# Splitting an x pair over two PSUM banks, five lead units, an earlier close of st0 and a last block in three column pieces, in a fused attention and feed-forward kernel

## The chip, the cores and the metric

One Trainium2 chip, one core of it. The metric is the device time of one execution in microseconds (us), which is about 1.7 us more than the span of the profile (287.74 for a profiled span of 286.0). Times are medians.

## The reference

Inputs are q, k, v of shape (8, 8, 576, 64) in float32, w_in (512, 2048), w_out (2048, 512) and beta (2048).

```python
q_s = softmax(q, axis=-1)             # over the head dimension
k_s = softmax(k, axis=2)              # over the sequence
kv  = einsum('bhsd,bhse->bhde', k_s, v)
x   = einsum('bhsd,bhde->bhse', q_s, kv)      # then (B*S, H*D) = (4608, 512)
h   = x @ w_in
out = (h * sigmoid(beta * h)) @ w_out
```

## The kernel before

The matmuls run in bf16. The 4608 tokens go through the feed-forward part in nine chunks of 512. A *unit* is 128 of the 2048 hidden columns of one chunk: four matmuls (k steps 0 to 3) into one PSUM bank, a tanh on ScalarE, and one VectorE instruction that makes g. The second matmul collects in *acc groups*: for each of the four 128-token slices st0 to st3 of a chunk, 16 matmuls go into one bank, which is then stored. `b_mm(m)` issues the next m acc matmuls of a fixed list, but none whose g is newer than four units (LAG). The attention of batch b+1 runs between the units of chunk b; batches 0 and 1 stand alone, in the code below. In the traces of this case each engine works in the order in which its instructions are written (in e7_exp_first below, one line moved up takes the Exp ahead of a copy on ScalarE, from 49.47 to 48.91 us).

```python
    def h_bank(n, i):                          # PSUM bank of unit i of chunk n
        if n == 0:
            return ("H0", "H1", "H2", "A0", "A1")[i % 5]
        if n == 1 and i < 6:
            return ("H0", "A0", "H1", "H2", "X0", "X1")[i]
        return f"H{(n * NJ + i + 2) % 3}"
    # the list of acc matmuls, chunk 1 and later
        for j in range(0, NJ, 4):
            for st in (0, 1):
                bq += [(n, st, j + m) for m in range(4)]
        for st in (2, 3, 4)[: 2 + (n == NCH - 1)]:
            bq += [(n, st, j) for j in range(NJ)]
    # ... (cut: b_mm, store) batch_1, its second half:
        b_mm(2)
        for i in range(4):
            unit_mm(1, i, 0, 1)                # k step 0 of units 0 to 3
        kv_pair(1, 3, "K")
        kv_mask(1, 3)                          # VectorE: gives kvp(1,3)
        x_mm(1, 2, "X0")
        q_exp(2, 0, 4)                         # ScalarE: Exp for batch 2
        x_out(1, 2, nc.scalar)
        q_exp(2, 4, 8)
        for i in range(4):
            unit_mm(1, i, 1, 2)
        x_mm(1, 3, "X1")
        x_out(1, 3, nc.vector, 0, 2)           # two copies out of one bank
        x_out(1, 3, nc.scalar, 2, 4)
        # ... (cut)
        for i in range(4):
            unit_mm(1, i, 2, 3)
```

In chunks 1 to 8 st0 and st2 share bank A1, st1 and st3 bank A0. In the last block st3 is done in two pieces of 256 columns, and the second is copied out by ScalarE and then VectorE, 128 columns each.

The softmax here doesn't subtract the row's maximum and nothing guards it: scores larger than these inputs give would overflow.

## Time and profile before

| | before |
|---|---|
| time, median of 3 runs | 288.08 us (287.67 to 288.71) |
| span of the profile | 286.0 us |
| TensorE busy | 97% |
| a 512-column matmul, start to start | 0.216 us |

Three lines of the page: the span, the engines' busy time, and the chain of waits by engine.

```profile
span 286.0 us, 4210 instructions
PE 277.5 (97%) x1445; PEld 132.4 (46%) x1472; DVE 158.9 (56%) x303; ACT 169.5 (59%) x275; POOL 79.2 (28%) x135
...
PE 83%; DMA 12%; POOL 1%; issue 1%; SPq 1%; ACT 1%; DVE 0%; ACTq 0%; POOLq 0%
```

TensorE is the bottleneck nearly everywhere, so the useful reading is not its busy share but its gaps. In a list of matmul starts, a 512-column matmul is followed by the next after 0.216 us; whatever is beyond that is a wait. (Exactly 0.216 more is taken as a missing record, unless another engine's record ends just before the later matmul starts.) The timeline has fewer gaps than that list: it gives a gap only when an engine was idle by its records, and there a 512-column matmul counts as busy for 0.38 us, 0.16 us longer than its slot. So add 0.16 us to a gap in brackets to have the time lost. (One gap, 0.45 us at 45.9 us for a cast of v, is left alone by the change.)

**Batch 0.** The timeline of TensorE, and of POOL (GpSimd), which casts the weights w_in. Columns: start, length, engine, line, operation, out and in, shapes, count, and in brackets the idle time and who ended it.

```profile
15.40 7.52 PE L405 MATMUL h<-xT,w_in_b 128*128 128x512 bf16 x31
23.25 6.65 PE L405 MATMUL h<-xT,w_in_b 128*128 128x512 bf16 x30 [0.32 <-POOL w_in_b L154]
```

```profile
16.38 1.18 POOL L154 TENSOR_SCALAR_AFFINE_SELECT w_in_b<-wi 128x512 bf16<-128x512 f32 x2 [0.75 <-DMA wi<-in_moe_w_in_dram]
...
21.21 1.05 POOL L154 TENSOR_SCALAR_AFFINE_SELECT w_in_b<-wi 128x1024 bf16<-128x1024 f32 x1 [0.67 <-DMA wi<-in_moe_w_in_dram]
```

POOL waited for the loads of w_in before each cast, and TensorE waited for POOL at 23.25. The stretch is paced by loads.

**Batch 1, second half.** TensorE, ScalarE (ACT) and VectorE (DVE):

```profile
49.07 1.03 PE L405 MATMUL h<-xT,w_in_b 128*128 128x512 bf16 x4
50.35 1.89 PE L405 MATMUL h<-xT,w_in_b 128*128 128x512 bf16 x8 [0.25 <-ACT xT L145]
52.23 0.39 PE L453 MATMUL acc<-w_out_b,g 128*128 128x512 bf16 x1
```

```profile
48.98 1.06 ACT L182 ACTIVATE Eq<-q 128x1024 bf16<-128x1024 f32 x1 [0.20 <-DMA q<-in_q_dram]
49.94 0.35 ACT L145 CAST xT<-x 128x256 bf16<-128x256 f32 x1
```

```profile
46.87 0.68 DVE L485 TENSOR_SCALAR o<-acc 128x512 f32<-128x512 f32 x1
47.97 0.17 DVE L320 RECIPROCAL rks<-kv 128x1 f32<-128x1 f32 x1 [0.43 <-PE kv L310]
...
49.27 0.42 DVE L159 CAST xT<-x 128x256 bf16<-128x256 f32 x1 [0.74 <-PE x L360]
```

The matmuls at 50.35 are the closing k steps of the lead units. They wait for ScalarE's half copy at 49.94, which stands behind an Exp of 1.06 us, and that Exp waited for a load of q: 0.415 us lost. The first acc matmul of chunk 1 (52.23) starts 0.154 us late, because g(1,0) had only just been made.

**A bank wait in the steady chunks.** TensorE near 104.6, then ScalarE:

```profile
104.63 1.18 PE L453 MATMUL acc<-w_out_b,g 128*128 128x512 bf16 x4
```

```profile
103.57 0.36 ACT L145 CAST xTt<-xt 128x256 bf16<-128x256 f32 x1
103.83 0.64 ACT L182 ACTIVATE Eq<-q 128x512 bf16<-128x512 f32 x1
104.36 0.60 ACT L487 ACTIVATE o<-acc 128x512 f32<-128x512 f32 x1
```

Four matmuls took 1.18 us in place of 1.03 (0.16 us lost), because st2 takes the bank of st0, whose store (104.36 to 104.95) is late behind a copy and an Exp. The same stands at 134.6 and 164.7, and 0.04 us at 74.7.

**The tail,** after the last matmul, which starts at 282.49:

```profile
282.85 0.28 ACT L479 ACTIVATE o_4b<-acc 128x128 f32<-128x128 f32 x1 [2.94 <-PE acc L453]
283.15 0.38 ACTq L482 DMA_DIRECT2D out_dram<-o_4b  x1
283.15 0.29 DVE L473 TENSOR_SCALAR o<-acc 128x128 f32<-128x128 f32 x1 [1.68 <-ACT o_4b L479]
```

VectorE's copy waits for ScalarE's copy of the same bank, and its DMA is the last to be issued.

### The profile page before, as it was taken

What the parts mean: (1) busy time and instruction counts of PE and PEld (TensorE: products, weight loads), DVE (VectorE), ACT (ScalarE), POOL (GpSimd) and SP (SyncE); (2) the same over time, 40 slices, a digit from 0 to 9 for tenths busy, and PEclk for the clock granted to TensorE, in tenths of its full rate; (3) what the DMA queues carried; (4) which work ended last, traced back from release to release, by engine and by line L of the source; (5) the groups of instructions that cost most, each with busy time, mean ns of one, the idle gap of its engine ahead of it and who ended that gap; (6) DMA issues with size and microseconds to landing.
All of it is one profiled execution on the core that took longest, in us unless ns stands there. A gap on an engine that the chain in (4) does not pass through costs nothing.

```text
span 286.0 us, 4210 instructions
## 1 busy us (share of the span) xinstructions
PE 277.5 (97%) x1445; PEld 132.4 (46%) x1472; DVE 158.9 (56%) x303; ACT 169.5 (59%) x275; POOL 79.2 (28%) x135
## 2 busy tenths in 40 slices
PE   8899999999999999999999999999999999999995
PEld 3443445454454444544454445444544444444444
DVE  5857346976856484747574666557553344433301
ACT  4767268956965588358835785568554544354421
POOL 7578953540531045103610271016100000000000
PEclk9999999999999999999999999999999999999999
DMA  7999999979589907990699059902400111031112
GB/s 234 353 364 386 381 355 353 361 207 360 142 205 351 161 37 194 364 198 2 161 359 269 2 135 310 308 2 89 99 37 0 73 39 38 0 75 39 37 73 73
DMA packets 55782, 51.67 MB, mean 181 GB/s; under 512 B 21184, under 2 KB 48208, under 8 KB 55760
## 3 DMA queue, kind: packets, MB, share of 16 engines
q1 hardware_dynamic: 55584, 51.33, 59.3%
q8 instruction: 11, 0.18, 0.3%
q14 instruction: 11, 0.09, 0.1%
q10 hardware_dynamic: 176, 0.07, 0.1%
HBM read 38.28 MB, written 9.44 MB: 167 GB/s over the span
## 4 chain that ended last, share of the span: by engine, by line
PE 83%; DMA 12%; POOL 1%; issue 1%; SPq 1%; ACT 1%; DVE 0%; ACTq 0%; POOLq 0%
PE h L405 40%; PE acc L453 39%; DMA v<-in_v_dram 5%; DMA q<-in_q_dram 4%; DMA wi<-in_moe_w_in_dram 3%; PE kv L283 2%; PE x L360 2%; SPq L132 1%; POOL w_out_b L154 0%; ACT Eq L182 0%; PE xt L375 0%; ACT th L417 0%; POOL w_in_b L154 0%; SPq L122 0%; POOL k L119 0%
## 5 line engine op out<-in xcount | busy, mean ns | idle before, releaser
L419 DVE SCALAR_TENSOR_TENSOR g<-th,h 128x512 bf16<-128x512 bf16 x144 | 98.2, 686 | 97.5 <-ACT th L417 97.3
L417 ACT ACTIVATE th<-h,beta_h 128x512 bf16<-128x512 f32 x144 | 98.4, 688 | 89.4 <-PE h L405 86.5
L453 PE MATMUL acc<-w_out_b,g 128*128 128x512 bf16 (+1 forms) x573 | 142.5, 373 | 0.9
L405 PE MATMUL h<-xT,w_in_b 128*128 128x512 bf16 x507 | 129.1, 379 | 0.9 <-POOL w_in_b L154 0.3
L405 PEld LDWEIGHTS <-w_in_b 128*128 128x128 bf16 x576 | 56.1, 98 | 69.2 <-POOL w_in_b L154 1.9
L453 PEld LDWEIGHTS <-g 128*128 128x128 bf16 x592 | 56.9, 98 | 62.7 <-issue 1.0
L194 POOL TENSOR_TENSOR Eq<-Eq,qz 128x512 bf16<-128x512 bf16 (+1 forms) x26 | 30.6, 1180 | 90.8 <-DVE qz L191 71.4
L182 ACT ACTIVATE Eq<-q 128x512 bf16<-128x512 f32 (+1 forms) x26 | 18.9, 727 | 10.7 <-DMA q<-in_q_dram 10.7
L190 DVE TENSOR_REDUCE qz<-Eq 128x8 f32<-128x512 bf16 (+1 forms) x27 | 21.0, 778 | 7.3 <-ACT Eq L182 7.3
L252 ACT ACTIVATE Ek<-k 128x640 bf16<-128x640 f32 (+1 forms) x30 | 22.9, 769 | 1.6 <-DMA k<-in_k_dram 1.3
L487 ACT ACTIVATE o<-acc 128x512 f32<-128x512 f32 x34 | 20.1, 595 | 6.1 <-PE acc L453 6.1
L154 POOL TENSOR_SCALAR_AFFINE_SELECT va<-v 128x256 bf16<-128x256 f32 (+1 forms) x55 | 20.7, 417 | 3.6 <-DMA v<-in_v_dram 3.6
L405 PE MATMUL h<-xTt,w_in_b 128*128 128x512 bf16 x62 | 16.2, 379 | 0.1
L360 PE MATMUL x<-qT,kvp 128*128 128x512 bf16 x32 | 12.0, 379 | 0.2
L145 ACT CAST xT<-x 128x512 bf16<-128x512 f32 (+1 forms) x19 | 10.6, 558 | 1.1 <-PE x L360 0.6
L159 DVE CAST xT<-x 128x512 bf16<-128x512 f32 (+1 forms) x15 | 9.7, 648 | 1.6 <-PE x L360 1.6
L236 POOL TENSOR_TENSOR Et<-Et,zt 128x512 bf16<-128x512 bf16 x4 | 4.2, 1043 | 22.4 <-ACT th L417 11.4
L154 POOL TENSOR_SCALAR_AFFINE_SELECT w_in_b<-wi 128x512 bf16<-128x512 f32 (+2 forms) x16 | 9.5, 617 | 3.1 <-DMA wi<-in_moe_w_in_dram 3.1
L544 PE MATMUL warm<-zero 128*128 128x512 bf16 x26 | 8.1, 471 | 1.3 <-DVE zero L507 1.3
L283 PEld LDWEIGHTS <-Ek 128*128 128x128 bf16 x120 | 7.8, 97 | 2.8
L283 PE MATMUL kv<-va,Ek 128*128 128x130 bf16 x120 | 8.8, 220 | 0.0
L154 POOL TENSOR_SCALAR_AFFINE_SELECT w_out_b<-wo 128x1024 bf16<-128x1024 f32 x8 | 8.3, 1043 | 1.4 <-DMA wo<-in_moe_w_out_dram 1.4
(53 smaller groups left out, 76.8 us busy)
## 6 DMA issues: line engine op xcount, KB each, us to landing
k<-in_k_dram SPq DMA_DIRECT2D x28, 320.0 KB, 6.5
v<-in_v_dram SPq DMA_DIRECT2D x26, 320.0 KB, 7.2
q<-in_q_dram SPq DMA_DIRECT2D x16, 512.0 KB, 5.2
out_dram<-o SPq DMA_DIRECT2D x31, 256.0 KB, 2.4
wo<-in_moe_w_out_dram SPq DMA_DIRECT2D x8, 512.0 KB, 10.8
wi<-in_moe_w_in_dram SPq DMA_DIRECT2D x7, 512.0 KB, 8.5
out_dram<-o SPq DMA_DIRECT2D x9, 128.0 KB, 2.3
k<-in_k_dram SPq DMA_DIRECT2D x4, 256.0 KB, 7.0
```

Source lines behind the costliest of these rows:

```text
L154: nc.gpsimd.affine_select(out=dst, in_=src, pattern=[[0, n]], base=0, channel_multiplier=0, compare_op=ALU.is_equal, fill=fill0,)
L182: nc.scalar.activation(Eq[b][:, :, h0:h1, :].rearrange("p t h d -> p h t d"), ld["q", b, hf][:, a : a + h1 - h0, :].rearrange("p h (t d) - ...
L190: nc.vector.tensor_reduce(qz[b][:, :, h], Eq[b][:, :, h, :], axis=AX.X, op=ALU.add)
L194: eng.tensor_tensor(Eq[b][:, t0:t1, h0:h1], Eq[b][:, t0:t1, h0:h1], qz[b][:, t0:t1, h0:h1].unsqueeze(3).to_broadcast((P, t1 - t0, h1 - h0, ...
L252: nc.scalar.activation(Ek[b][:, :, h0:h1, :].rearrange("p t h d -> p h t d"), ld["k", b, hf][:, a : a + h1 - h0, :].rearrange("p h (t d) - ...
L283: nc.tensor.matmul(kvs[b, j // 2][:, j % 2, :], Ek[b][:, t, 2 * j : 2 * j + 2, :].rearrange("p h d -> p (h d)"), va[b % 2][:, t, j, :], st ...
L360: nc.tensor.matmul(xps[b, j][:], kvp[b][:, j, :], qT[b][:, :, j, :], start=True, stop=True)
L405: nc.tensor.matmul(hs[n, i][:], w_in_b[:, kt, i * P : (i + 1) * P], rhs_a(n, kt), start=(kt == 0), stop=(kt == KT - 1),)
L417: nc.scalar.activation(th[:], h[:], ACTF.Tanh, scale=beta_h[:, i : i + 1])
L419: nc.vector.scalar_tensor_tensor(out=g[:], in0=th[:], scalar=1.0, in1=h[:], op0=ALU.add, op1=ALU.mult)
L453: nc.tensor.matmul(acc[n, st][:, c0:c1], gs[n, j][:, min(st, 3) * P : (min(st, 3) + 1) * P], w_out_b[:, j, c0:c1], start=(j == 0), stop=(j ...
L487: nc.scalar.activation(o[:], acc[n, st][:], ACTF.Copy, scale=0.5)
```

## The change

The intent: take away these waits. (a) The last x pair of batches 0 and 1 is computed into two banks, so that two engines can copy at once. (b) In batch 1 the last key-value pair comes two matmuls earlier, and the last x pair behind two matmuls of k step 1 in place of four; the store of acc(0,3) goes behind its mask, the second Exp behind the half copies, and five units instead of four lead. (c) st0 closes sooner: two groups of st1 (eight acc matmuls) stand between its close and st2, where it was one, so that st2 finds its bank free. (d) The last block is done in pieces of 256, 128 and 128 columns in three banks. Cut to its core:

```diff
+    def x_split(b, j, na, nb):
+        # ... (cut)
+        for i, (n, eng) in enumerate(((na, nc.vector), (nb, nc.scalar))):
+            t = slice(2 * i, 2 * i + 2)
+            ps = bank(n, [P, 2, P], F32, f"x{b}_{j}_{i}")
+            nc.tensor.matmul(ps[:], kvp[b][:, j, :], qT[b][:, t, j, :], start=True, stop=True)
+            cast(eng, xT[b][:, j, t], ps[:])
 # h_bank
-            return ("H0", "H1", "H2", "A0", "A1")[i % 5]
-        if n == 1 and i < 6:
-            return ("H0", "A0", "H1", "H2", "X0", "X1")[i]
-        return f"H{(n * NJ + i + 2) % 3}"
+            return ("H1", "H2", "A0", "A1", "H0")[i % 5]
+        if n == 1 and i < 7:
+            return ("H0", "A0", "H1", "H2", "A1", "X0", "X1")[i]
+        return f"H{(n * NJ + i + 1) % 3}"
 # the list of acc matmuls
-        for j in range(0, NJ, 4):
-            for st in (0, 1):
-                bq += [(n, st, j + m) for m in range(4)]
-        for st in (2, 3, 4)[: 2 + (n == NCH - 1)]:
+        for st, j in ((0, 0), (1, 0), (0, 4), (1, 4), (0, 8), (0, 12), (1, 8), (1, 12)):
+            bq += [(n, st, j + m) for m in range(4)]
+        for st in (2, 3, 4, 5)[: 2 + 2 * (n == NCH - 1)]:
 # b_mm: st0 and st2 now in A0, st1 and st3 in A1; columns of the last block
+        if n == NCH - 1 and st > 2:
+            return ((0, DM // 2), (DM // 2, 3 * DM // 4), (3 * DM // 4, DM))[st - 3]
 # batch 0
-    x_mm(0, 3, "K")
-    x_out(0, 3, nc.vector, 0, 2)
-    x_out(0, 3, nc.scalar, 2, 4)
-    LEAD = (2, 4)
+    x_split(0, 3, "K", "H0")
+    LEAD = (2, 5)
 # batch 1
-        for i in range(4):
+        for i in range(2):
             unit_mm(1, i, 0, 1)
         kv_pair(1, 3, "K")
         kv_mask(1, 3)
+        store(0, 3)
+        for i in range(2, 4):
+            unit_mm(1, i, 0, 1)
         x_mm(1, 2, "X0")
         q_exp(2, 0, 4)
         x_out(1, 2, nc.scalar)
+        for i in range(2):
+            unit_mm(1, i, 1, 2)
+        x_split(1, 3, "X1", "K")
         q_exp(2, 4, 8)
-        for i in range(4):
+        for i in range(2, 4):
             unit_mm(1, i, 1, 2)
-        x_mm(1, 3, "X1")
-        x_out(1, 3, nc.vector, 0, 2)
-        x_out(1, 3, nc.scalar, 2, 4)
+        unit_mm(1, 4, 0, 2)
 # ... (cut: acc(0,3) is no longer stored right behind its last matmul;
 # k steps 2 and 3 of units 0 to 4 follow unit by unit; no b_mm after unit 4;
 # the store of the last block: pieces 1 and 2 on VectorE, piece 3 on ScalarE and its own DMA queue)
```

More of the change, by code (lines that the diff above doesn't have):

```diff
@@ L362, in x_mm @@
         )
+    def x_split(b, j, na, nb):
+        if b not in xT:
+            xT[b] = atn.tile([P, KT, NT, P], BF16, tag="xT", name=f"xT{b}")
+        for i, (n, eng) in enumerate(((na, nc.vector), (nb, nc.scalar))):
[3 more added lines that the diff above has]
+            cast(eng, xT[b][:, j, t], ps[:])
     def x_out(b, j, eng, t0=0, t1=NT):
@@ L439, with cols @@
     done_a = [-1]
+    def cols(n, st):
+        if n == NCH - 1 and st > 2:
+            return ((0, DM // 2), (DM // 2, 3 * DM // 4), (3 * DM // 4, DM))[st - 3]
+        return 0, DM
     def b_mm(m):
@@ L446, in b_mm @@
             if j == 0:
-                name = (f"A{1 - st % 2}", ("X1", "K", "A0", "A1", "")[st])[n == 0]
+                name = ("X1", "K", "A0", "A1")[st] if n == 0 else f"A{st % 2}"
+                if st == 5:
+                    name = "X0"
                 acc[n, st] = bank(name, [P, DM], F32, f"acc{n}_{st}")
-            c0, c1 = 0, DM
-            if n == NCH - 1 and st > 2:
-                c0, c1 = (st - 3) * DM // 2, (st - 2) * DM // 2
+            c0, c1 = cols(n, st)
             nc.tensor.matmul(
@@ L459, in b_mm @@
             )
-            if j == NJ - 1:
+            if j == NJ - 1 and (n, st) != (0, 3):
                 store(n, st)
@@ L468, in store @@
             rows = out[(B - 1) * S : (B - 1) * S + CH, :].rearrange("(p t) e -> p t e", t=NT)
-            for i in range(st - 2):
-                w = DM // 2 // (st - 2)
-                c0 = (st - 3) * DM // 2 + i * w
-                if st == 3 or i:
-                    nc.vector.tensor_scalar(
-                        o[:, c0 : c0 + w], acc[n, st][:, c0 : c0 + w], 0.5, None, op0=ALU.mult
-                    )
-                    nc.sync.dma_start(rows[:, 3, c0 : c0 + w], o[:, c0 : c0 + w])
-                else:
-                    o2 = osp.tile([P, DM], F32, tag="o", name=f"o{n}_{st}b")
-                    nc.scalar.activation(
-                        o2[:, 0:w], acc[n, st][:, c0 : c0 + w], ACTF.Copy, scale=0.5
-                    )
-                    nc.scalar.dma_start(rows[:, 3, c0 : c0 + w], o2[:, 0:w])
+            c0, c1 = cols(n, st)
+            if st < 5:
+                nc.vector.tensor_scalar(
+                    o[:, c0:c1], acc[n, st][:, c0:c1], 0.5, None, op0=ALU.mult
+                )
+                nc.sync.dma_start(rows[:, 3, c0:c1], o[:, c0:c1])
+            else:
+                nc.scalar.activation(o[:, c0:c1], acc[n, st][:, c0:c1], ACTF.Copy, scale=0.5)
+                nc.scalar.dma_start(rows[:, 3, c0:c1], o[:, c0:c1])
             return
@@ L656, in batch_1 @@
         x_out(1, 2, nc.scalar)
+        for i in range(2):
+            unit_mm(1, i, 1, 2)
+        x_split(1, 3, "X1", "K")
         q_exp(2, 4, 8)
-        for i in range(4):
+        for i in range(2, 4):
             unit_mm(1, i, 1, 2)
-        x_mm(1, 3, "X1")
-        x_out(1, 3, nc.vector, 0, 2)
-        x_out(1, 3, nc.scalar, 2, 4)
+        unit_mm(1, 4, 0, 2)
         q_sum(2, 0, 4)
         q_div(2, 0, NT, nc.gpsimd, 0, 4)
-        for i in range(4):
-            unit_mm(1, i, 2, 3)
     hooks: dict = {}
@@ L715 @@
         for i in range(NJ):
-            unit_a(n, i, 3 if n < 2 and i < LEAD[n] else 0)
+            unit_a(n, i, 3 - n if n < 2 and i < LEAD[n] else 0)
             for f in hooks.get((n, i), []):
                 f()
-            if n:
+            if n and (n, i) != (1, 4):
                 b_mm(4)
```

## The prediction

> **What bounds the kernel.** TensorE. On the page, PE is busy 97% of a 286.0 us span, PEclk is at full speed in every slice, and the chain of waits is 83% PE. In the timeline a 512-column matmul follows the one before every 0.216 us; I read each start gap beyond that as a wait (gaps of exactly 0.216 are missing records). From 52.5 us to the last matmul (ends 282.8) I find only about 0.5 us of waits. Everything to be gained lies in four places.
>
> 1. Batch 0, 15 to 23 us. The last x pair (one bank) is copied by VectorE (15.60 to 16.03), and only then by ScalarE (16.06 to 16.44), so the closing matmuls of units 0 and 1 start 0.22 us late. The Trainium skill (PSUM - Partial Sum Buffer, "PSUM bank collisions raise a hardware error") says two engines may not read one bank at once; the trace agrees in that ScalarE starts 0.03 us after VectorE ends. Two banks remove this wait. But unit 2 starts at 17.05 because POOL's w_in_b cast ends at 17.00, itself begun when its DMA landed; the same at 22.32 and 23.25 (gap 0.49). These are set by the loads. Expected gain: 0.
>
> 2. Batch 1, 42 to 52 us. Gaps of 0.29, 0.16, 0.45 (casts of v, Eq normalisation) are before the changed part and stay. Then 0.415 us at 49.9: the second half of the last x pair waits for a 1.06 us Exp on ScalarE and for VectorE, whose chain had been held by the 0.68 us store of acc(0,3). And 0.154 us at 52.07: the first acc matmul of chunk 1 waits for g(1,0) (ends 52.17). The change puts the key-value pair two matmuls earlier, the store behind its mask, the Exp behind the half copy, and unit 4 (20 matmuls of k steps 0 to 3) before the first acc matmul. Replayed with the trace's durations, xT(1,3) is ready near 49.3 and wanted at 49.7; g(1,0) is ready near 51.8 and wanted at 52.5. Gain 0.55.
>
> 3. Steady chunks. Gaps of 0.16 at 104.6, 134.6, 164.7 and 0.04 at 74.7: st2 takes the bank of st0 only 8 matmuls after st0 closed, with ScalarE late (xT tail cast, Exp, then the 0.60 us store). Closing st0 two groups sooner, more than 12 matmuls ahead, removes them. Gain 0.5. The acc queue lags four matmuls more, which moves work, not its amount. st1 now meets st3's bank after 8 matmuls (1.73 us), next to no ScalarE cast: fine.
>
> 4. Tail, after the last matmul: ScalarE copy 0.28, then VectorE copy 0.29 of the same bank, then SyncE's DMA (issue at 283.47, landed 285.1). Now one ScalarE copy and its own DMA issue (before: at 283.15). Gain 0.3. The 256-column piece becomes two 128-column pieces: 16 matmuls at 0.109 become 32 at 0.056 (the trace's pace for 128 columns), cost 0.05.
>
> **Sum:** 0 + 0.55 + 0.5 + 0.25 = 1.3 us of 288.08. Predicted 286.8 us, 80% range 285.9 to 287.8. Faster by over 2%: 1%; within 2%: 98%; slower by over 2%: 1%.
>
> **What would show it.** Span near 284.7; unit 2 of chunk 0 still near 17.05 and the 0.49 gap near 22.5 still there; no PE gap at 49 to 52 us and none between acc matmuls near 104, 134, 164; only a ScalarE copy after the last matmul, and the end about 3.0 us after it instead of 3.2.
>
> **What would make it wrong.** A new wait: units of chunk 1 taking PSUM banks still held by the moved store (unit 4 in A1, slack 0.2 us), ScalarE late in chunk 1 where acc matmuls are fewer, weight loads limiting the 128-column pieces (then up to 1.3 us more, from 97 ns per load), or w_in landing at other times.

## More of the kernel before

All runs told here were with a granted TensorE clock of 0.99 or 1.00.

VectorE's store of acc(0,3) (46.87) is over at 47.55, and VectorE then idles 0.43 us until the key-value pair's matmuls are done, so it holds nothing up.

**Start of chunk 2** (no gap here before the change; shown because one comes).

```profile
67.61 0.38 PE L360 MATMUL x<-qT,kvp 128*128 128x512 bf16 x1
67.83 1.03 PE L453 MATMUL acc<-w_out_b,g 128*128 128x512 bf16 x4
68.69 1.03 PE L405 MATMUL h<-xT,w_in_b 128*128 128x512 bf16 x4
```

## The result, and the profile after

| | before | after |
|---|---|---|
| time, median of 4 runs each, same rounds | 287.93 us | 287.21 us |
| range | 287.67 to 288.71 | 287.02 to 287.61 |
| span of the profile | 286.0 us | 285.5 us |

The ratio is 0.9972, with a 95% interval of 0.995 to 0.9995: about 0.8 us faster, and by the interval anything from 0.1 to 1.4 us. A ratio is the mean time of one kernel's fast runs over that of the other's of the same rounds, so not quite the ratio of the medians in the table.

```profile
span 285.5 us, 4276 instructions
PE 279.2 (98%) x1490; PEld 133.3 (47%) x1490; DVE 157.8 (55%) x303; ACT 169.5 (59%) x275; POOL 79.4 (28%) x135
...
PE 82%; DMA 14%; POOL 1%; SPq 1%; issue 0%; ACT 0%; POOLq 0%; ACTq 0%
```

Batch 0, TensorE and POOL. The wait at 16.71 stands where the two-bank copies have made room, and the waits before 22.67 and 23.61 are the loads'. The bracket at 22.67 names VectorE; but that bank had been freed by g of unit 3 at 20.06, and what ended at 22.61 was POOL's cast of the 1024-column weights. POOL had waited 1.36 us for them.

```profile
16.71 5.35 PE L415 MATMUL h<-xT,w_in_b 128*128 128x512 bf16 x24 [0.20 <-POOL w_in_b L154]
22.67 0.60 PE L415 MATMUL h<-xT,w_in_b 128*128 128x512 bf16 x2 [0.61 <-DVE g L429]
23.61 6.65 PE L415 MATMUL h<-xT,w_in_b 128*128 128x512 bf16 x30 [0.33 <-POOL w_in_b L154]
```

```profile
21.57 1.04 POOL L154 TENSOR_SCALAR_AFFINE_SELECT w_in_b<-wi 128x1024 bf16<-128x1024 f32 x1 [1.36 <-DMA wi<-in_moe_w_in_dram]
```

Batch 1: TensorE runs through from 48.79 to 53.3 without a gap. ScalarE's half copy is the second of the two at 48.55, ahead of the Exp; VectorE's store now stands behind the mask.

```profile
48.79 0.38 PE L371 MATMUL x<-qT,kvp 128*128 128x256 bf16 x2
49.00 4.05 PE L415 MATMUL h<-xT,w_in_b 128*128 128x512 bf16 x18
52.89 0.59 PE L467 MATMUL acc<-w_out_b,g 128*128 128x512 bf16 x2
```

```profile
48.55 1.02 ACT L145 CAST xT<-x 128x512 bf16<-128x512 f32 x2
49.47 1.06 ACT L182 ACTIVATE Eq<-q 128x1024 bf16<-128x1024 f32 x1
```

```profile
48.38 0.68 DVE L494 TENSOR_SCALAR o<-acc 128x512 f32<-128x512 f32 x1
49.10 0.42 DVE L159 CAST xT<-x 128x256 bf16<-128x256 f32 x1
```

Start of chunk 2, TensorE, then the copies of xT(2) on VectorE and ScalarE:

```profile
67.41 0.38 PE L360 MATMUL x<-qT,kvp 128*128 128x512 bf16 x1
67.62 0.38 PE L467 MATMUL acc<-w_out_b,g 128*128 128x512 bf16 x1
67.84 1.36 PE L415 MATMUL h<-xT,w_in_b 128*128 128x512 bf16 x4
```

```profile
67.64 0.68 DVE L159 CAST xT<-x 128x512 bf16<-128x512 f32 x1
```

```profile
68.19 0.58 ACT L145 CAST xT<-x 128x512 bf16<-128x512 f32 x1
```

This is new. Before, four acc matmuls (67.83 to 68.69) stood between the last x matmul and the first unit of chunk 2; now there is one, and the unit takes 1.36 us in place of 1.03, because its k steps 2 and 3 wait for the copies that end at 68.32 and 68.77.

The bank wait is gone (four matmuls in 1.03 us again), and after the last matmul, which now starts at 282.20, there is one copy:

```profile
103.85 1.03 PE L467 MATMUL acc<-w_out_b,g 128*128 128x512 bf16 x4
```

```profile
282.50 0.28 ACT L490 ACTIVATE o<-acc 128x128 f32<-128x128 f32 x1 [2.98 <-PE acc L467]
282.81 0.38 ACTq L491 DMA_DIRECT2D out_dram<-o  x1
```

From the last matmul's start to the end it is 3.26 us, before 3.53.

**The sum,** read from the starts of the same instructions in the two profiles:

| stretch | predicted | profiles (before to after) |
|---|---|---|
| batch 0, to the first acc matmul | 0 | +0.36 (29.73 to 30.09) |
| batch 1 | -0.55 | -0.57 (0.415 and 0.154 gone) |
| start of chunk 2 | 0 | +0.33 (new) |
| bank waits | -0.5 | -0.52 (3 x 0.16 and 0.04 gone) |
| last block and tail | -0.25 | -0.18 |
| all | -1.3 | -0.58; the spans differ by 0.57 |

Two terms have to be explained: the loss in batch 0, and the loss at the start of chunk 2.

### The profile page after: what moved, and what is told of

Its sections match the earlier page's. It is cut to its first block, busy times and chain, and to the rows that moved or that the text cites. A ratio compares the mean times of both kernels' runs of the same rounds, so it can differ in the third digit from the quotient of the medians.

```text
span 285.5 us, 4276 instructions
## 1 busy us (share of the span) xinstructions
PE 279.2 (98%) x1490; PEld 133.3 (47%) x1490; DVE 157.8 (55%) x303; ACT 169.5 (59%) x275; POOL 79.4 (28%) x135
## 4 chain that ended last, share of the span: by engine, by line
PE 82%; DMA 14%; POOL 1%; SPq 1%; issue 0%; ACT 0%; POOLq 0%; ACTq 0%
PE acc L467 39%; PE h L415 39%; DMA wo<-in_moe_w_out_dram 4%; DMA q<-in_q_dram 4%; PE kv L283 2%; DMA k<-in_k_dram 2%; DMA v<-in_v_dram 2%; DMA wi<-in_moe_w_in_dram 2%; PE x L360 2%; SPq L124 0%; PE xt L385 0%; POOL va L154 0%; SPq L122 0%; PE kv L310 0%; ACT xT L145 0%
## 5 line engine op out<-in xcount | busy, mean ns | idle before, releaser
L467 PE MATMUL acc<-w_out_b,g 128*128 128x512 bf16 (+2 forms) x608 | 145.0, 368 | 0.0
L360 PE MATMUL x<-qT,kvp 128*128 128x512 bf16 x30 | 11.2, 379 | 0.2
L553 PE MATMUL warm<-zero 128*128 128x512 bf16 x27 | 9.2, 509 | 1.2 <-DVE zero L516 1.2
```

Source lines behind the costliest of these rows:

```text
L360: nc.tensor.matmul(xps[b, j][:], kvp[b][:, j, :], qT[b][:, :, j, :], start=True, stop=True)
L467: nc.tensor.matmul(acc[n, st][:, c0:c1], gs[n, j][:, min(st, 3) * P : (min(st, 3) + 1) * P], w_out_b[:, j, c0:c1], start=(j == 0), stop=(j ...
```

## The experiments

My theory: the loss in batch 0 is scatter in the landing of loads and not the change's doing; the loss at chunk 2 comes with the new order of the acc groups; the gain in batch 1 comes from the moves, not from the two banks. Rivals: the split of batch 0 causes its loss; the five lead units cause the loss at chunk 2; the two banks, or the store's place, give the gain in batch 1. Ratios are to the kernel before, measured in the same rounds on the same chip. All eleven kernels gave correct results.

### 1. The change's parts alone

**e1_batch1**: only (b), with the split in batch 1, the banks for five lead units and the swap of A0 and A1; the order of the acc groups, batch 0 and the last block as before.

> Only the batch 1 part of the change (key-value pair earlier, store behind its mask, Exp behind the half copy, split banks, five lead units). Theory: the two TensorE gaps of 0.415 and 0.154 us between 49 and 53 us go, no new gap appears in chunk 1, and the time falls by 0.55 us (ratio 0.998). The gaps of 0.16 us in the later chunks (near 104, 134, 164 us) and the 3.53 us from the last matmul's start to the end stay. Rival (the gain of batch 1 is only pushed to a later wait): gaps of the same size turn up between 55 and 75 us and the time is that of before. The start of unit 8 of chunk 0, set by the loads, lies anywhere from 22.2 to 22.8 us, though nothing in batch 0 has changed.

Measured: 287.55 us, ratio 0.9985 (0.997 to 0.9999). Both gaps are gone, none is new, the three bank waits of 0.16 us and the tail of 3.54 us stay. As the theory said. Batch 0, untouched, ends 0.3 us later than in the profile of before (first acc matmul at 30.04).

**e2_order**: only (c).

```diff
-        for j in range(0, NJ, 4):
-            for st in (0, 1):
-                bq += [(n, st, j + m) for m in range(4)]
+        for st, j in ((0, 0), (1, 0), (0, 4), (1, 4), (0, 8), (0, 12), (1, 8), (1, 12)):
+            bq += [(n, st, j + m) for m in range(4)]
```

> Only the order of the acc groups (st0 closes two groups sooner, in every chunk from 1 on). Theory: it is a gain and a loss: the four waits for a bank (0.04 + 3 x 0.16 us) go, and a new wait of about 0.33 us appears where chunk 2 starts (near 68 us), because only one acc matmul instead of four is ready after the last unit of chunk 1 to cover the copies of xT. Net 0.1 to 0.2 us faster (ratio 0.9995), not clear of the noise. Rival (the wait at 68 us came from the five lead units, not from the order): no gap at 68 us here, and 0.5 us faster.

Measured: 287.70 us, ratio 0.9998 (0.9982 to 1.0013). TensorE at the start of chunk 2 in this run:

```profile
68.10 1.36 PE L405 MATMUL h<-xT,w_in_b 128*128 128x512 bf16 x4
```

The 1.36 us unit is there with four lead units too: the order brings it. The bank waits near 104, 134 and 164 us are gone. The gain and the loss nearly cancel.

**e3_tail**: only (d).

> Only the last block in column pieces of 256, 128, 128. Theory: the last matmul starts 0.05 to 0.1 us later (32 matmuls of 128 columns for 16 of 256), the stretch from the last matmul's start to the end shrinks from 3.53 to 3.26 us, net 0.2 us faster. Rival (weight loads of 98 ns set the pace of the 128-column pieces): the last matmul starts 1.3 us later, and the time is about 1 us longer.

Measured: 287.70 us, ratio 0.9989 (0.9975 to 1.0003); the tail is 3.26 us. The 128-column matmuls follow each other after 0.056 us, though each loads its own weights for 98 ns; the rival is out. This profile also showed something about batch 1: its old wait for the half copy was 0.75 us here, in place of 0.415, since the Exp ahead of it waited longer for its load of q.

```profile
49.61 1.06 ACT L182 ACTIVATE Eq<-q 128x1024 bf16<-128x1024 f32 x1 [0.54 <-DMA q<-in_q_dram]
```

In e2_order and e4_batch0 the same wait was 0.22 us. So what (b) takes away is not a fixed 0.415 us: it is 0.22 us that the two copies in turn cost even where the Exp is out of the way (see e9_exp_only), and on top a dependence of TensorE on that load.

**e4_batch0**: only the split in batch 0.

```diff
-            return ("H0", "H1", "H2", "A0", "A1")[i % 5]
+            return ("H1", "H2", "A0", "A1", "H0")[i % 5]
 ...
-    x_mm(0, 3, "K")
-    x_out(0, 3, nc.vector, 0, 2)
-    x_out(0, 3, nc.scalar, 2, 4)
+    x_split(0, 3, "K", "H0")
```

> Only the split x pair of batch 0 over two banks. Theory: the closing matmuls of units 0 and 1 of chunk 0 start 0.22 us sooner, but unit 2 starts when the cast of its weights ends, and unit 8 when the 1024-column weights have landed; the time is unchanged (within 0.2 us). Rival A (the split itself makes the later weights land later, as the 0.36 us lost in the changed kernel's profile suggest): unit 8 starts at 22.6 us or later and the time is 0.3 us longer. Rival B (the 0.22 us are gained): 0.2 us faster.

Measured: 288.02 us, ratio 1.0004 (0.999 to 1.0018): nothing gained, none of it lost clear of the noise. TensorE:

```profile
17.11 5.35 PE L415 MATMUL h<-xT,w_in_b 128*128 128x512 bf16 x23 [0.16 <-POOL w_in_b L154]
22.76 0.61 PE L415 MATMUL h<-xT,w_in_b 128*128 128x512 bf16 x2 [0.29 <-POOL w_in_b L154]
```

Units 0 and 1 close earlier, and unit 2 waits for POOL's cast. Unit 8 starts at 22.76, late as rival A expected; what speaks against rival A are the kernels with an untouched batch 0. The first acc matmul (the end of batch 0's stretch) started at 29.73, 30.04, 30.06, 30.02 and 30.36 us in the five profiles without the split, and at 30.09, 30.17, 30.54, 30.16, 29.98, 30.08, 31.19 and 29.95 us in the eight with it. The medians, 30.04 and about 30.13, are 0.09 us apart, with a scatter of several tenths in each. The profile of before was the fastest of its kind, so the +0.36 us in the table is read as mostly luck of that profile. That is not shown: with five and eight profiles that scatter so, and with the time's interval from 0.3 us faster to 0.5 us slower, an effect of the split of a few tenths either way is not ruled out. The load of the 1024-column weights itself landed between 20.53 and 21.94 us (median 21.16) without the split, and between 21.38 and 22.61 us (median 21.55) with it; this leans to rival A, but by the first acc matmul only 0.09 us are left of it.

### 2. What in batch 1 gives the gain

Three kernels put one move back into the changed kernel.

**e6_one_bank**

```diff
-        x_split(1, 3, "X1", "K")
+        x_mm(1, 3, "X1")
+        x_out(1, 3, nc.vector, 0, 2)
+        x_out(1, 3, nc.scalar, 2, 4)
```

> The changed kernel, but the last x pair of batch 1 in one bank again, copied in two halves one after the other; all moves stay. Theory: ScalarE's half ends near 50.0 us where the changed kernel has 49.6, but its first reader (k step 3 of unit 0) comes at 50.08, so no gap opens between 49 and 53 us and the time is that of the changed kernel: in batch 1 the moves did it, not the two banks. Rival (the split does it): a gap of 0.3 us or more there.

Measured: 287.36 us, ratio 0.9977 (0.9961 to 0.9992). TensorE runs from 49.33 without a gap at the closing k steps; only 0.05 us are lost ahead of the first acc matmul (it takes bank A0 from unit 1, and starts 0.05 us after g(1,1) ends at 53.00). In this profile the two banks are worth that 0.05 us, no more. But the one bank leaves nothing to spare: ScalarE's half copy ended at 50.15 and its reader started at 50.20, where the changed kernel had 49.58 and 50.08.

**e7_exp_first**

```diff
-        x_split(1, 3, "X1", "K")
         q_exp(2, 4, 8)
+        x_split(1, 3, "X1", "K")
```

> The changed kernel, but the Exp of batch 2's second half stands before the split copies in ScalarE's queue again, as in before. Theory: this is what ties TensorE to that load: a gap of 0.4 to 1.0 us opens at k step 3 of unit 0 (near 50.1 us), as long as the 1.06 us Exp and the landing of q make it; about 0.5 us slower than the changed kernel. Rival (the store was what held the chain): no gap.

Measured: 287.44 us, ratio 0.9982 (0.9965 to 1.0). The gap opens, 0.33 us (0.16 idle and the 0.16 of the matmul's own length), a little under the expected 0.4, for the load of q was early in this profile and the Exp did not wait for it; what is left is the length of the Exp:

```profile
50.29 2.97 PE L415 MATMUL h<-xT,w_in_b 128*128 128x512 bf16 x13 [0.16 <-ACT xT L145]
```

The time is slower than the changed kernel's 0.9972 in the expected direction, but the intervals overlap; the gap in the trace is the evidence.

**e8_store_first**

```diff
+        store(0, 3)
         kv_pair(1, 3, "K")
         kv_mask(1, 3)
-        store(0, 3)
```

> The changed kernel, but VectorE stores acc(0,3) ahead of the mask again. Theory: with the key-value pair two matmuls earlier the mask still ends near 48.6 us, just before the split x pair is wanted at 48.79, so no gap of more than 0.1 us opens and the time is that of the changed kernel. Rival (the store was the cause of the 0.4 us): a gap of 0.3 us or more near 48.8 us.

Measured: 287.21 us, ratio 0.9967 (0.9954 to 0.9981); no gap between 48 and 53 us. The store's place did not matter once the key-value pair came earlier. My prediction had listed it among the causes, though in the profile of before VectorE was already idle for 0.43 us behind the store.

**e9_exp_only**: the kernel before, with the Exp alone moved.

```diff
         x_out(1, 2, nc.scalar)
-        q_exp(2, 4, 8)
 ...
         x_out(1, 3, nc.scalar, 2, 4)
+        q_exp(2, 4, 8)
```

> The kernel before with one line moved: the Exp of batch 2's second half behind the half copies of the last x pair of batch 1. Theory: the wait at k step 3 of unit 0 (0.22 to 0.75 us in the profiles so far) settles at its floor of 0.2 us, set by VectorE's chain, but the Exp now delays the first tanh, so g(1,0) is ready only near 52.5 us and the wait of the first acc matmul of chunk 1 grows from 0.155 to 0.6 us or so: the wait is moved, not removed, and the time is that of before within 0.3 us. Rival (the Exp's place alone is the gain of batch 1): both gaps together under 0.4 us and 0.4 us faster.

Measured: 288.49 us, ratio 1.0014 (1.0001 to 1.0027). TensorE:

```profile
49.69 2.97 PE L405 MATMUL h<-xT,w_in_b 128*128 128x512 bf16 x12
53.03 0.39 PE L453 MATMUL acc<-w_out_b,g 128*128 128x512 bf16 x1 [0.37 <-DVE g L419]
```

The first wait is at its floor of 0.22 us (within the group at 49.69), and the second has grown from 0.154 to 0.53 us: the Exp now stands ahead of the first tanh, so g(1,0) is late. Moved, not removed: the two waits together are 0.75 us, where they were 0.57 in the profile of before and 0.37 in those of e2_order and e4_batch0. The kernel is 0.4 us slower by the ratio, a little outside the 0.3 us expected. The floor of 0.22 us comes from TensorE's own order: the x pair is computed only behind four matmuls of k step 1 (49.47 us), then VectorE and ScalarE copy its one bank in turn. In the changed kernel the matmuls of the fifth lead unit and of unit 5 fill the time until g(1,0) is there (52.89 for the first acc matmul, no wait).

### 3. Versions that might be faster still

**e5_order_from_2**: the new order of the acc groups only from chunk 2 on.

```diff
-        for st, j in ((0, 0), (1, 0), (0, 4), (1, 4), (0, 8), (0, 12), (1, 8), (1, 12)):
+        order = ((0, 0), (1, 0), (0, 4), (1, 4), (0, 8), (0, 12), (1, 8), (1, 12))
+        for st, j in sorted(order, key=lambda a: (a[1], a[0])) if n == 1 else order:
```

> The changed kernel, but chunk 1 keeps the old order of the acc groups; st0 closes sooner from chunk 2 on. Theory: four acc matmuls again stand between the last unit of chunk 1 and the first of chunk 2, so the 0.33 us gap near 68 us goes, and the bank waits near 104, 134 and 164 us stay away (at most one gap of 0.04 us near 74 us comes back). 0.3 us faster than the changed kernel, ratio to before about 0.996. Rival (the copies of xT(2) are late for another reason): the gap near 68 us stays.

Measured: 286.96 us, ratio 0.9958 (0.9945 to 0.997), with no gap at the start of chunk 2, where four acc matmuls stand again:

```profile
68.01 1.03 PE L468 MATMUL acc<-w_out_b,g 128*128 128x512 bf16 x4
```

The bank waits stay away, but for 0.04 us at 74.9. This is the fastest version by its median. It and the changed kernel were not timed in the same rounds and their intervals overlap, so that it is 0.3 us faster rests on the trace, where 0.33 us of wait are gone and 0.04 are back. e8_store_first, which has the waits of the changed kernel, was timed in the same session: its mean is 287.21 us and that of e5 286.94, 0.27 us less, with runs that overlap.

**e10_fill** and **e11_fill_late**: e5 with two acc matmuls moved into the 0.43 us that TensorE waits in batch 1 for a cast of v, first ahead of the x matmuls, then behind them.

```diff
 # e10_fill
-        b_mm(2)
+        b_mm(4)
         x_mm(1, 0, "X0")
         x_mm(1, 1, "K")
 # e11_fill_late
         x_mm(1, 1, "K")
+        b_mm(2)
 # both: the two taken away further down
-        b_mm(2)
```

> The version with the old order in chunk 1, and the two acc matmuls that stood behind the third key-value pair of batch 1 put ahead of it, where TensorE waits 0.43 us for GpSimd's cast of v. Theory: that gap is filled and everything after it comes 0.43 us sooner, as none of the later copies of batch 1 was closer than that to its reader: ratio to before 0.994 to 0.995. Rival (the copies, the q load or the first tanh hold the next step at its old time): a new gap of up to 0.4 us between 47 and 53 us and no gain over the version without it.

> As the previous attempt to fill the 0.43 us gap, but the two acc matmuls stand behind the two x matmuls of batch 1, not ahead of them, so that ScalarE's copies of x start no later than in the version without the filling. Theory: the earlier attempt only moved the wait because it made the x matmuls, and with them both copies, 0.43 us later; now the gap is filled, no new one of more than 0.1 us appears between 46 and 53 us, and the time falls to a ratio of 0.9945 or so. Rival (the next step is held by something else, as the q load or the casts of v): the gap turns up again between 46 and 50 us.

Measured: e10 287.18 us, ratio 0.9967 (0.9953 to 0.998); e11 287.12 us, ratio 0.9974 (0.9961 to 0.9988). Neither beats e5. In e10 the copies of x start later with the x matmuls, and the wait turns up behind them (0.34 and 0.42 us). In e11 it turns up at the last key-value pair (0.32 us):

```profile
47.22 0.46 PE L310 MATMUL kv<-va,Ek 128*128 128x130 bf16 x5 [0.16 <-ACT xT L145]
```

The bracket is right here: the pair goes into bank K, which ScalarE is still copying x out of (46.57 to 47.16). My expectation had looked at data only and not at the bank. The rivals of both were right that the gap turns up again; what holds the step is neither the q load nor a cast of v, but a copy, and in e11 through its bank. Of the 0.43 us only 0.1 was gained.

## Why the prediction was right, and where it was off

The time, 287.21 us, lies in the range (285.9 to 287.8), and "within 2%" was right. That alone says little: the range began 0.1 us under the 287.93 us of before, so a gain of almost any size up to 2 us would have fallen into it. The gain was 0.8 us by the ratio, not 1.3.

- **TensorE bounds, and only its gaps count:** right. The gaps of TensorE, the last block and the tail add up to 0.58 us, and the spans differ by 0.57.
- **Batch 0 gains nothing:** right as far as the noise lets one see (e4_batch0). Unit 2 waited for POOL's cast, as said. The 0.36 us that the profile lost there are most likely scatter of the loads (not shown, see e4_batch0), which the prediction knew only as "w_in landing at other times".
- **Batch 1 gains 0.55 us:** right in size (0.57) and the replayed times held: xT(1,3) was ready at 49.58 (said 49.3) and wanted at 50.08, the first acc matmul had no wait. But of the causes named, the two banks gave 0.05 us (e6), and the store's place nothing (e8): the step "whose chain had been held by the 0.68 us store" was wrong, for in the profile of before VectorE had ended the store 0.43 us before it could go on. The Exp's place is needed (e7: without it the gap opens) and is not enough (e9: alone it only moves the wait). That the earlier key-value and x pairs and the fifth unit are the rest of it is argued from their times in the trace; none was taken away alone. The old wait also varies, from 0.22 to 0.75 us in profiles with the old batch 1.
- **Steady chunks gain 0.5 us:** right for the bank waits (0.52). The step that failed is the sentence "The acc queue lags four matmuls more, which moves work, not its amount." The amount is the same, but at the end of chunk 1 the queue has no more than what LAG lets through, and closing st0 sooner means that g of units 12 to 15 is wanted earlier than it may be used. So one acc matmul, not four, is left to cover the copies of xT(2): 0.33 us (e2_order has it, e5_order_from_2 does not). The prediction's list of dangers has "ScalarE late in chunk 1 where acc matmuls are fewer", but the sum gave it nothing.
- **Tail gains 0.25 us:** 0.18 by the profiles, 0.3 by e3_tail's ratio, whose interval holds both. The 128-column pieces cost 0.05 us, as said.

So 1.3 less 0.33 at chunk 2 and 0.07 in the tail leaves 0.9 us, against 0.8 measured; with an interval of 0.1 to 1.4 us, that they agree so well is luck.

## What to carry to other kernels

When TensorE bounds, list its gaps one by one and ask of each what else is just behind the thing that you remove: a faster copy ahead of a load that has not landed, or an Exp moved from one wait to the next, gains nothing. A queue of filler work that is limited by how new its data may be runs dry at the seams; an order that suits the steady state should be tried apart from the first round. And for differences of a few tenths of a microsecond, compare the same stretch in many profiles, untouched ones too, before you explain it.

## What the Trainium skill lacked or had wrong

- "TensorE: Matmul & The Clock Gate", section "Back-to-back issue gap", gives about 131 ns per matmul of N=512 and 81 ns of N=128 as the sustained pace of streams of weight loads and matmuls, and calls the 216 ns formula one for isolated matmuls. Here the streams, each matmul with its own weight load, ran at 216 ns for 512 columns (560 acc matmuls in the profile after) and at 56 ns for 128 columns (the 32 of the last block): the formula of that section holds, the sustained figures do not.
- "PSUM — Partial Sum Buffer", section "PSUM bank collisions raise a hardware error", says that two engines may not read one bank at once. The traces agree in that the second half copy always followed the first (0.03 us after it in batch 0 before the change); no run tried a collision. What keeping to it costs a kernel is on no page: here the second half copy starts one half copy of 0.42 us later, and in e6_one_bank that was 0.05 us of TensorE's time.
- "DMA: Bandwidth & Descriptors", section "Queues, rings and completion order", says that completion is not first in, first out per issuing engine; no run here tests that. No page says how much the landing of the same load scatters from run to run: POOL's cast of the 1024-column weights, which stands behind that load and at its earliest behind the cast before it, started between 20.59 and 22.67 us in the thirteen profiles (the load landed 8.02 to 9.59 us after its issue), and the second Exp of batch 2, behind its load of q, at 48.98 us in the profile of before and at 49.61 us in that of e3_tail, with the same batch 1 code.
